# Long-convolution taps in two halves, small elementwise steps on GpSimd, two channels per table product, plain first loads

## The chip, the cores and the metric

The kernel runs on one core of a Trainium2 chip. A core has a matrix engine (TensorE, PE in the profile, with its weight loads as PEld), a vector engine (VectorE, DVE), a scalar engine (ScalarE, ACT), GpSimd (POOL), and a queue that only issues transfers (SyncE, SP). The metric is the device time of one execution in microseconds, the median of the runs.

## The reference, cut to what matters

Two layers work on the same input x of 2048 tokens by 512 channels, and a gate per token mixes them. Layer A is attention in four segments of 512 tokens with 32 heads of 16, plus a memory that is carried from segment to segment. Layer B is a state-space model that is applied as a long convolution.

```python
# A: for each of the four segments
logits = einsum('bhqd,bhkd->bhqk', qs, ks) * scale + mask
a_dot = softmax(logits) @ vs
pq = phi(qs)                       # t + 1 if t > 0 else exp(t)
a_mem = (pq @ M) / (pq @ z + 1e-6)
o = g * a_mem + (1 - g) * a_dot
M, z = M + phi(ks)^T vs, z + sum(phi(ks))
# B: taps of 2048 steps for each of 512 channels, then a convolution
P = exp(dt * A * l)
K = einsum('dn,dnl,dn->dl', Cc, P, dt * Bc).real
y = irfft(rfft(x, 4096) * rfft(K, 4096))[:2048] + x * Dskip
# mix
out = sigmoid(x . gate_w) * A(x) + (1 - sigmoid(x . gate_w)) * B(x)
```

## The kernel before

The kernel states its operations with their operands, and a planner inside it, `Sched`, gives each a place in the instruction stream of its engine. A sort key sets the order: a base key by stage plus an offset from the table `ORDER`, by the operation's tag. An operation made by `evac` may go to ACT or DVE; the planner picks one with its own costs. The streams are then fixed. Engines wait for each other by semaphores, and each stream runs in order. `MASKS` says for each of 32 groups of heads and five steps whether the causal mask is added by PE into the scores (a product with `negm`) or multiplied on DVE after the exponential.

**Start.** `praw` holds the six parameter arrays of layer B, loaded by transposing DMAs (one row of x or of a parameter becomes a column). `do_xT` loads each segment of x in the same way, in four pieces. The identity, log_dt and two weights are issued from ACT's queue (`early`).

**Powers and tables (layer B's taps).** `ssm_prep` forms z = exp(dt·A) for all channels and states, `ssm_powers` squares it again and again for ten powers and writes each as bf16 with a swapped and negated copy (lines 904 and 324/325), so that a complex product is two products and one sum. `tables(c)`, for each of four sets of 128 channels, builds a table F of 20 powers (steps 1 to 1800) and a table G of 32 powers (multiples of 8) by `cmul`, with lines 1328, 1330 and 1333 on DVE. PE then multiplies the tables over the 128 states: for each channel two matmuls (real and imaginary part) with 32 columns of G as weights and 20 of F moving, 1024 in all, four channels at once on four column strips of the array. The copies go to `kex` and by small DMAs to `KTT`, the taps.

**Attention.** For each segment and each two groups of four heads: `project` (q, k, and `ko`, a copy of k with the even heads cleared, line 1121; from segment 1 on also phi(q), lines 1125 to 1128), `seg_state` (phi(k) and the sums of the memory, lines 1075 to 1078), `group` (five steps of scores into PSUM, exponential on ACT at line 1169, mask at line 1178, products with v), `ophase` (division, lines 1229 to 1258, and a turn through DRAM for segments 0 to 2), `oproj` (output weights).

**Convolution.** `x_level1` transforms x over one part of its index and writes it to `scr_Z` in DRAM. `tail` then runs over 16 frequency groups of 128 frequencies: the taps' spectrum `PK` (five products over the five parts of the taps, for the real and for the imaginary part), copied to `K3`; the spectrum of x `PX`, copied to `Xs`; a complex product on DVE in four steps (lines 1425, 1427, 1430); the first step back `PI`, copied to `V` and by DMA into `V2`. Loads of the constants `c_D` and of `scr_Z` are issued from POOL. The last stage adds attention's part (`aj`), multiplies with `G2T` and writes the output.

Line 820 is the helper through which nearly all matmuls go, 317 that of all DMAs, 324 and 325 those of the copies on ACT and on DVE.

Of the kernel before, what the change touches and what calls it, by code (L numbers as in the profile page):

```python
# [8 lines left out]
BF16 = mybir.dt.bfloat16  # L9
# [7 lines left out]
    'c_ident': (-302.654696, 118.5323), 'c_mk': (25.0776717, 31.1201), 'c_negm': (117.240337, 15.88946),  # L17
    'c_mask': (82.9696732, 148.73681), 'c_ones': (219.06097, 69.01982), 'c_W1': (101.972009, -1.91191),
    'c_G2': (152.510402, 64.12832), 'ld0': (-159.6066, -3.90904), 'ld1': (-178.483329, -24.17737),
    'ld2': (-92.104013, -32.87557), 'ld3': (-67.6677276, 9.94046), 'ld4': (-16.8975543, -9.33976),  # L20
    'ld5': (-4.87843354, -20.81767), 'ldt': (-255.221528, 18.97994), 'ldw0.3': (-120.015437, 20.25449),
    'ldw0.4': (-107.069287, 54.02795), 'ldw0.5': (-74.7706898, 55.68128), 'ldw50': (143.580885, 71.64248),
    'ldbd': (146.873282, -3.63178), 'ldc': (75.9548493, -139.44835), 'prep': (241.088944, 76.53782),
    'xT0': (-135.794939, 94.16918), 'powA0': (-118.34783, 47.94242), 'powA1': (293.056234, 56.59733),
    'powA2': (35.605867, 26.1545), 'powA3': (85.9672701, 3.55388), 'powA4': (-134.9878, 64.48103),
    'powA5': (-26.1625064, 59.29796), 'powA6': (-133.006553, -36.0664), 'powA7': (-142.410857, 92.25773),
    'powA8': (-143.096642, 54.65219), 'powA9': (-10.832777, 2.7911), 'cbA': (-135.566534, 76.23563),
    'powB0': (-38.6484402, 86.47076), 'powB1': (5.73197339, 19.09463), 'powB2': (-13.5842481, 50.52935),
    'powB3': (-134.626625, -55.3453), 'powB4': (-158.321758, -62.26012), 'powB5': (-189.375726, 81.95324),
    'powB6': (-80.3854645, -2.33938), 'powB7': (-23.5296877, 39.40937), 'powB8': (-69.1011372, 80.90111),  # L30
    'powB9': (-110.631611, 11.18354), 'cbB': (-43.7416241, -8.34436), 'gate0': (-83.6885532, -16.32166),
    'gate': (1.11235274, 54.68591), 'proj0.0': (-19.4170356, -12.54463), 'tok0': (-79.3938344, 28.87985),
    'state0': (2.03704365, 1.9988), 'grp0.0.0': (-9.77190791, 56.39033), 'grp0.0.1': (-15.5684214, 42.32006),
    'oph0.0': (16.6476846, 20.40017), 'proj0.1': (-31.4882721, 74.16452), 'grp0.1.0': (-22.0475879, 127.40729),
    'grp0.1.1': (-23.8762151, 61.87469), 'oph0.1': (-9.68776635, -98.76067), 'proj0.2': (13.8209713, 33.73148),
    'grp0.2.0': (-3.0729207, -42.9295), 'grp0.2.1': (-4.41502647, 85.93088), 'oph0.2': (-0.110628858, -73.44253),
    'proj0.3': (-3.65051527, 62.72309), 'grp0.3.0': (-157.898249, 69.86549), 'grp0.3.1': (15.8097506, 82.05476),
    'oph0.3': (1.58288994, 45.63335), 'oproj0': (-119.328043, -32.2024), 'xT1': (152.351944, 17.87594),
    'proj1.0': (9.25225381, 119.56925), 'tok1': (-10.2534902, 33.782), 'state1': (2.65910208, -104.20105),
    'grp1.0.0': (-90.77533, -81.81367), 'grp1.0.1': (2.11773201, -114.61486), 'oph1.0': (-2.73170943, -41.40325),  # L40
    'proj1.1': (1.88542876, 58.71674), 'grp1.1.0': (-50.654272, 32.17712), 'grp1.1.1': (2.9233842, 75.51506),
    'oph1.1': (-10.8350984, -95.48593), 'proj1.2': (1.82372045, 0.09674), 'grp1.2.0': (-40.190034, 101.48513),
    'grp1.2.1': (6.26606409, 118.92692), 'oph1.2': (-0.686318884, -116.61307), 'proj1.3': (0.240651948, 30.33776),
    'grp1.3.0': (-46.8631087, 31.58558), 'grp1.3.1': (4.26113506, 92.65595), 'oph1.3': (16.5142754, -29.00959),
    'oproj1': (-191.3713, -3.8356), 'xT2': (96.7803542, 126.17717), 'proj2.0': (2.03309827, 56.77169),
    'tok2': (4.1651971, -119.61949), 'state2': (5.77674239, -0.78865), 'grp2.0.0': (-34.2653109, -9.07765),
    'grp2.0.1': (-5.67836684, 97.22657), 'oph2.0': (-250.752907, -56.23876), 'proj2.1': (6.5976729, 122.63846),
    'grp2.1.0': (-4.50294478, 30.38303), 'grp2.1.1': (4.81855669, 106.57043), 'oph2.1': (15.6722872, -167.79793),
    'proj2.2': (-0.107249989, 90.02738), 'grp2.2.0': (-195.487509, 48.11696), 'grp2.2.1': (-5.26881311, 86.02262),
    'oph2.2': (10.7493513, -113.28868), 'proj2.3': (-7.49951321, 95.76044), 'grp2.3.0': (5.83724795, 81.21215),  # L50
    'grp2.3.1': (-32.6003357, 74.62712), 'oph2.3': (-34.0930078, -105.98926), 'oproj2': (-42.4160159, -7.99807),
    'xT3': (290.268696, 20.01374), 'proj3.0': (0.804501688, 7.58942), 'tok3': (5.05705523, 9.43832),
    'grp3.0.0': (-16.6209468, 115.71971), 'grp3.0.1': (-94.3400298, 75.95984), 'oph3.0': (34.3743725, -53.14357),
    'proj3.1': (-5.34871522, 74.39357), 'grp3.1.0': (31.8837621, -11.25205), 'grp3.1.1': (-311.171354, -14.40604),
    'oph3.1': (-107.203104, -69.86356), 'proj3.2': (72.9991952, 27.09956), 'grp3.2.0': (20.1657102, -6.85936),
    'grp3.2.1': (-59.0699755, -14.4919), 'oph3.2': (88.4879918, -147.86965), 'proj3.3': (79.119397, 97.40507),
    'grp3.3.0': (5.32990942, 126.86441), 'grp3.3.1': (61.7741135, -22.60438), 'oph3.3': (-130.287319, -60.50239),
    'oproj3': (-33.6345043, -45.3022), 'tab0': (-0.0762501383, 297.60803), 'tab1': (-3.85305439, 267.74954),
    'tab2': (-0.288638216, 266.94455), 'tab3': (9.72332812, 324.53498), 'xl1': (-134.058337, -22.9888),
    'tailload': (-94.6594205, 59.19368), 'K0': (-16.3376241, 5.32994), 'K1': (44.0845545, -26.15755),  # L60
    'K2': (9.34286849, 3.42233), 'K3': (45.356053, 32.70617), 'K4': (39.7158986, -80.36254),
    'K5': (59.226848, -13.36243), 'K6': (-175.798043, 23.12264), 'K7': (-52.4250027, -83.01271),
    'K8': (-81.0202091, -26.97997), 'K9': (70.2758069, 29.6753), 'K10': (11.2349379, 25.06385),
    'K11': (-5.3357892, -30.98575), 'K12': (-72.5533468, 4.35854), 'K13': (83.6417633, 0.11429),
    'K14': (94.4918388, -109.55134), 'K15': (132.562985, 53.83523), 'fin': (-85.9153477, -15.31372),
    'pre0': (169.976104, -25.42423), 'fin0': (91.9347751, 60.72191), 'pre1': (-73.3504102, -61.54381),
    'fin1': (115.799027, 117.99035), 'fin2': (125.104546, 66.48059), 'fin3': (213.962257, 170.74892),
}
MASKS = [2, 0, 0, 0, 0, 0, 0, 0, 0, 28, 0, 0, 0, 1, 0, 0, 16, 16, 14, 4, 0, 28, 0, 1, 3, 15, 31, 31, 15, 13, 26, 20]
# [122 lines left out]
class Sched:  # L192
# [141 lines left out]
    def schedule(self):  # L334
# [23 lines left out]
        dma_free = 4.5  # L358
# [221 lines left out]

def c_mm(n, k=1):
    return k * (0.014 + n / 2300.0)
# [3 lines left out]
def fft_consts():  # L586
# [21 lines left out]
    N1 = np.zeros((128, 16, 2, 2, 64))  # L608
    for t in range(16):
        for pi in range(2):  # L610
            pp = 2 * t + pi
            c_, s_ = cs[pp].T, sn[pp].T
            rs = slice(64 * pi, 64 * pi + 64)
            N1[rs, t, 0, 0] = c_
            N1[rs, t, 1, 0] = -s_
            N1[rs, t, 0, 1] = s_
            N1[rs, t, 1, 1] = c_
    G2 = np.zeros((128, 2, 128))
    for t in range(16):
        for pi in range(2):  # L620
            for c in range(2):
                for i in range(4):
                    a_ = ang[:, 2 * t + pi]
                    G2[v2_row(t) + 4 * (4 * (pi if c == 0 else 1 - pi) + i), c, 4 * ((4 * j + i) % 32) + (4 * j + i) // 32] = 2.0 / 4096 * (np.cos(a_) if c == 0 else -np.sin(a_))
# [3 lines left out]
def v2_row(t):  # L628
    return 64 * (t >> 3) + 32 * ((t >> 2) & 1) + (t & 3)


F_EXP = [1, 3, 5, 7, 2, 4, 6, 8, 258, 260, 262, 264, 516, 520, 772, 776, 1032, 1288, 1544, 1800]
# [3 lines left out]
def dft_const():  # L636
    lq = (np_bf16_bits(np.arange(2048, dtype=np.float32)).astype(np.uint32) << 16).view(np.float32).astype(np.int64)
    where = {}
    for f, fe in enumerate(F_EXP):
        for g, ge in enumerate(G_EXP):  # L640
            assert fe + ge not in where
            where[fe + ge] = (f % 5, 4 * g + f // 5)
    assert set(lq[1:].tolist()) == set(where)
    D = np.zeros((128, 16, 5, 2, 128))
    t = np.arange(16)[:, None, None]
    pi = np.arange(2)[None, :, None]
    q = np.arange(64)[None, None, :]
    f = (2 * t + pi + 64 * q).reshape(16, 128)
    for l in range(1, 2048):
        kt, r = where[int(lq[l])]  # L650
# [922 lines left out]
```

## Time and profile before

| what | value |
|---|---|
| median of three runs | 357.27 us (355.72 to 368.35) |
| the profiled execution's own time | 355.81 us |
| its span in the profile | 354.0 us |
| mean granted PE clock | 0.946 |
| all DVE two-input table steps (lines 1328, 1330, 1333) | 52 of each, 657 ns mean |
| exponentials on ACT (line 1169) | 160, 1037 ns mean |
| mask products on DVE (line 1178) | 43, 369 ns mean |
| copies of 1024 from PSUM | 47 on ACT at 1028 ns, 16 on DVE at 1219 ns |
| copies of 512 from PSUM | 81 on ACT at 617 ns, 21 on DVE at 685 ns |
| first DVE product of the parameters | starts at 9.81 us |
| last table product on PE | about 241 us |
| last frequency group's product on DVE | ends near 332 us |

A busy share is an average over stages of different kinds, so the stages are read one by one. The time of an instruction is from its start to its end; on PE the ends are modelled, so that a burst of matmuls is better measured by its length than by the sum of its instructions. "Issue" is time in which an engine waited for nothing that the profile shows. A mean of a line covers all its sizes unless the size is given.

### The profile page before, as it was taken

How to read it: one execution, taken by the hardware profiler on the slowest of the kernel's cores; microseconds unless marked ns; L12 is line 12 of the kernel's file. 1: busy time of each engine (PE TensorE's matmuls, PEld its weight loads, DVE VectorE, ACT ScalarE, POOL GpSimd, SP SyncE). 2: the span in 40 equal slices, each digit the busy share in tenths (PEclk: the TensorE clock that was granted, in tenths of full speed). 3: DMA queues.
4: the chain of work that ended last, by engine and by line, in shares of the span. 5: the costliest groups of instructions: out<-in, count | busy, mean ns of one | idle time of the engine just before them, and what ended most of it. 6: DMA issues, size and time to landing. Idle time of an engine off the chain costs nothing.

```text
span 354.0 us, 8296 instructions
## 1 busy us (share of the span) xinstructions
PE 298.4 (84%) x3409; PEld 125.1 (35%) x3409; DVE 274.6 (78%) x667; ACT 285.9 (81%) x387; POOL 17.3 (5%) x39
## 2 busy tenths in 40 slices
PE   0669887688939999999889999987999999999691
PEld 0223332233424432543335543353343333344240
DVE  2788999999848998399998899942877778986220
ACT  2798999899937998998999898945999768665472
POOL 2000000000000000000010000000001120100000
PEclk9996999699987996999999999998999999999897
DMA  7879021013592474801006210251134656533342
GB/s 173 172 161 109 1 91 30 3 54 99 197 148 76 136 176 126 205 23 30 2 8 186 71 44 17 59 167 37 40 102 181 217 181 211 149 114 93 109 156 90
DMA packets 43117, 37.56 MB, mean 106 GB/s; under 512 B 30568, under 2 KB 35944, under 8 KB 42216
## 3 DMA queue, kind: packets, MB, share of 16 engines
q1 hardware_dynamic: 39016, 22.18, 25.8%
q0 software_dynamic: 2720, 13.63, 12.3%
q10 hardware_dynamic: 1344, 1.21, 1.5%
q8 instruction: 27, 0.44, 0.5%
q14 instruction: 10, 0.08, 0.1%
HBM read 17.74 MB, written 9.44 MB: 77 GB/s over the span
## 4 chain that ended last, share of the span: by engine, by line
DVE 38%; PE 33%; ACT 20%; issue 4%; DMA 3%; SPq 0%
PE psum L820 33%; ACT sb L1169 11%; ACT sb L324 6%; DVE sb L1330 5%; DVE sb L1328 5%; DVE sb L1333 5%; DVE sb L325 4%; DMA sb<-in_B_A_im_dram 2%; ACT sb L327 2%; DVE sb L1232 2%; DVE sb L1252 1%; DVE sb L1178 1%; DVE sb L1430 1%; DVE sb L1425 1%; DMA sb<-sb 1%
## 5 line engine op out<-in xcount | busy, mean ns | idle before, releaser
L820 PE MATMUL psum<-sb 128*32 128x20 bf16 (+13 forms) x3233 | 287.7, 276 | 46.5 <-DMA sb<-in_A_x_dram 11.7
L820 PEld LDWEIGHTS psum<-sb 128*128 128x128 bf16 (+4 forms) x3233 | 115.0, 97 | 215.2 <-issue 88.4
L1169 ACT ACTIVATE sb<-psum 128x1024 bf16<-128x1024 f32 x160 | 157.5, 1037 | 7.7 <-PE psum L820 7.1
L324 ACT ACTIVATE sb<-psum 128x512 bf16<-128x512 f32 (+2 forms) x134 | 97.7, 753 | 37.6 <-PE psum L820 36.7
L325 DVE CAST sb<-psum 128x512 bf16<-128x512 f32 (+2 forms) x39 | 34.9, 894 | 16.0 <-PE psum L820 15.8
L1328 DVE TENSOR_TENSOR sb<-sb 128x512 bf16<-128x512 bf16 (+3 forms) x52 | 34.0, 657 | 0.1
L1333 DVE TENSOR_TENSOR sb<-sb 128x512 bf16<-128x512 bf16 (+3 forms) x52 | 33.8, 658 | 0.1
L1330 DVE TENSOR_TENSOR sb<-sb 128x512 bf16<-128x512 bf16 (+3 forms) x52 | 33.6, 658 | 0.0
L1178 DVE TENSOR_TENSOR sb<-sb 128x512 bf16<-128x512 bf16 (+1 forms) x43 | 15.6, 369 | 4.6 <-ACT sb L1169 4.4
L324 ACT ACTIVATE sb<-sb 128x256 bf16<-128x256 bf16 (+1 forms) x32 | 15.4, 500 | 1.1 <-DVE sb L904 1.0
L1425 DVE TENSOR_TENSOR sb<-sb 128x1024 bf16<-128x1024 bf16 x16 | 10.8, 683 | 6.5 <-ACT sb L324 5.2
L1430 DVE TENSOR_TENSOR sb<-sb 128x512 bf16<-128x512 bf16 x32 | 13.2, 417 | 0.6
L1229 DVE RECIPROCAL sb<-psum 128x32 f32<-128x32 bf16 x16 | 5.6, 350 | 10.4 <-PE psum L1226 10.4
L317 POOL DMA_DIRECT2D sb<-c_D x16 | 8.6, 538 | 91.4 <-PE psum L820 66.5
L327 ACT ACTIVATE sb<-psum,sb 128x512 bf16<-128x512 f32 x13 | 8.6, 687 | 4.7 <-PE psum L820 4.7
L1427 DVE TENSOR_TENSOR sb<-sb 128x1024 bf16<-128x1024 bf16 x16 | 10.9, 683 | 0.2 <-ACT sb L324 0.2
L1232 DVE TENSOR_TENSOR sb<-psum,sb 128x512 bf16<-128x512 bf16 x16 | 10.9, 682 | 0.0
L1226 PE MATMUL psum<-sb 128*128 128x128 bf16 x128 | 9.8, 220 | 0.1
L1252 DVE TENSOR_TENSOR sb<-psum,sb 128x256 bf16<-128x256 f32 x24 | 9.2, 415 | 0.1
L325 DVE COPY sb<-sb 128x256 bf16<-128x256 bf16 x17 | 3.9, 247 | 6.0 <-PE psum L820 6.0
L1226 PEld LDWEIGHTS psum<-sb 128*128 128x128 bf16 x128 | 7.5, 98 | 2.5 <-ACT sb L324 0.7
L1125 ACT ACTIVATE sb<-sb 128x512 bf16<-128x512 bf16 x12 | 8.0, 666 | 0.1
(71 smaller groups left out, 142.1 us busy)
## 6 DMA issues: line engine op xcount, KB each, us to landing
sb<-c_D POOLq DMA_DIRECT2D x16, 320.0 KB, 4.4
scr_Z<-sb SPq DMA_DIRECT2D x16, 256.0 KB, 2.0
sb<-scr_Z POOLq DMA_DIRECT2D x4, 1024.0 KB, 5.5
sb<-sb SPq DMA_DIRECT2D x15, 256.0 KB
sb<-in_A_x_dram POOLq DMA_DIRECT2D x4, 512.0 KB, 5.2
scr_obuf<-sb SPq DMA_DIRECT2D x12, 128.0 KB, 1.9
scr_abuf<-sb SPq DMA_DIRECT2D x12, 128.0 KB, 1.7
sb<-scr_abuf SPq DMA_DIRECT2D x3, 512.0 KB, 6.1
```

Source lines behind the costliest of these rows:

```text
L324: fa = lambda e: e.activation(dst(), src(), ACT.Copy)
L325: fd = lambda e: e.tensor_copy(dst(), src())
L327: fa = lambda e: e.activation(dst(), src(), ACT.Copy, scale=scale())
L820: mm = lambda e, o_, l, r_, st, sp, **kw: e.matmul(o_, lhsT=l, rhs=r_, start=st, stop=sp, skip_group_check=True, **kw)
L1169: op("ACT", c_act(1024), lambda e, P=P, pT=pT: e.activation(ap(pT, n=1024), ap(P, n=1024), ACT.Exp, scale=0.25), r=[P], w=[pT])
L1178: o_ = op("DVE", c_tt(128 * len(offs)), lambda e, pT=pT, dims=dims: e.tensor_tensor(ap(pT, dims=dims + [[1, 128]]), ap(pT, dims=dims + [[1 ...
L1226: i = e.transpose(ap(P, tb * 256 + gi * 128, n=128), ap(ra[gi], tb * 128, n=128), ap(ident, n=128))
L1232: op("DVE", c_dps(512), lambda e: e.tensor_tensor(ap(o1, dims=[[128, 4], [16, 8], [1, 16]]), ap(P, dims=[[256, 4], [32, 8], [1, 16]]), ap( ...
L1328: op("DVE", ct, lambda e: e.tensor_tensor(run(tile, ne, dst, 1), run(tile, ne, src, sstep), pwv(0), ALU.mult), r=rd + [pw], w=wr + [tile])
L1330: op("DVE", ct, lambda e: e.tensor_tensor(run(t2, n, 0, 1), run(tile, ne, src, sstep), pwv(1), ALU.mult), r=rd + [pw], w=[t2])
L1333: op("DVE", max(c_tt(256 * n), 0.4), lambda e: e.tensor_tensor(D_(), D_(), ap(t2, n * 128, [[-n * 128, 2], [2 * n, 64], [1, 2 * n]]), ALU. ...
L1430: op("DVE", c_tt(512), lambda e, Y=Y, Tt=Tt, c=c, alu=alu: e.tensor_tensor(ap(Y, 512 * c, n=512), ap(Y, 512 * c, n=512), ap(Tt, 512 * c, n ...
```

## The change

1. **First loads.** A_re, A_im and the first segment of x come by plain DMAs and are transposed on PE; the two weights that were issued from ACT's queue are issued from SP's.
2. **Copies, minima and maxima on GpSimd.** The negated and the swapped copy of each power, `ko`, the clips of phi(q) and phi(k), the first entries of the tables, and the second product of `cmul` where it makes one or two powers.
3. **Tables and their products.** F is ordered by odd and even steps. One matmul takes 64 columns of G (two neighbouring channels) as weights and 40 of F; of its 64×40 results the two blocks of a channel with itself are kept. 512 matmuls in three pieces for each set of channels.
4. **Taps to frequency.** Frequency f and the one half a period on have the same sums over even taps and opposite sums over odd taps. So the even part (`PK[0]`, four products) and the odd part (`PK[1]`, four) are formed once for two groups; their sum and their difference are two DVE steps from PSUM and SBUF. `tail` runs over eight double groups; its four DVE steps become two of 2048 and two of 1024; the constants N1, D and G2 are ordered to suit.
5. **Masks and filler.** `MASKS` has 81 steps on DVE where it had 43. `FILLS` puts one unused 128×512 matmul ahead of the scores in 55 steps.
6. **Order.** All of `ORDER` is new, and with it the choice of ACT or DVE for the copies.

```diff
-MASKS = [2, 0, 0, 0, 0, 0, 0, 0, 0, 28, 0, 0, 0, 1, 0, 0, 16, 16, 14, 4, 0, 28, 0, 1, 3, 15, 31, 31, 15, 13, 26, 20]
+MASKS = [0, 1, 2, 3, 0, 20, 11, 24, 15, 24, 11, 9, 10, 8, 15, 19, 21, 17, 4, 21, 16, 29, 17, 1, 27, 23, 31, 31, 31, 30, 14, 24]
+FILLS = [0, 3, 10, 3, 0, 23, 27, 4, 4, 4, 8, 7, 19, 16, 9, 10, 14, 25, 2, 12, 0, 0, 22, 0, 10, 4, 0, 0, 6, 10, 29, 26]
...
-F_EXP = [1, 3, 5, 7, 2, 4, 6, 8, 258, 260, 262, 264, 516, 520, 772, 776, 1032, 1288, 1544, 1800]
+F_EXP = [1, 3, 5, 7, 2, 6, 258, 262, 4, 8, 260, 264, 516, 520, 772, 776, 1032, 1288, 1544, 1800]
...
+            if wi < 2:
+                S.dma(lambda T=T: ap(T, n=512), lambda wi=wi: prm[wi].rearrange("(p k) n -> p (k n)", k=4), 131072, w=[T], key=(-1.6, -1.7)[wi])
...
+                        for k in range(4):
+                            i = e.transpose(ap(P, t2 * 512 + k * 128, n=128), ap(xks, (2 * hb + t2) * 512 + k * 128, n=128), ap(ident, n=128))
...
-                op("DVE", c_ts4(256), lambda e, dst=dst: e.tensor_scalar(dst(384, 1), dst(256, 1), -1.0, None, ALU.mult), r=parts, pw=parts)
-                S.evac(lambda dst=dst: dst(0, 1), lambda dst=dst: dst(128, 1), 256, r=parts, pw=parts, sb=True)
+                op("POOL", c_pl(256), lambda e, dst=dst: e.tensor_scalar(dst(384, 1), dst(256, 1), -1.0, None, ALU.mult), r=parts, pw=parts)
+                op("POOL", c_pl(256), lambda e, dst=dst: e.tensor_copy(dst(0, 1), dst(128, 1)), r=parts, pw=parts)
...
-            op("DVE", c_ts4(512), lambda e: e.tensor_scalar_min(ap(ek, n=512), ap(ek, n=512), 1.0), w=[ek])
+            op("POOL", c_pl(512), lambda e: e.tensor_scalar_min(ap(ek, n=512), ap(ek, n=512), 1.0), w=[ek])
...
+                    if FILLS[gidx] >> si & 1:
+                        mm(e, ap(P, n=512), ap(kT, n=128), ap(qT, n=512), True, True)
...
-                op("DVE", ct, lambda e: e.tensor_tensor(run(t2, n, 0, 1), run(tile, ne, src, sstep), pwv(1), ALU.mult),
+                op(*(("POOL", c_pl2(256 * n)) if n < 3 else ("DVE", ct)), lambda e: e.tensor_tensor(run(t2, n, 0, 1), run(tile, ne, src, sstep), pwv(1), ALU.mult),
...
-                                    i = mm(e, ap(P, sl * NF, n=NF, p0=32 * dq, np_=32), ap(G, (1 - cc) * GPL + (dl // 2) * 2 * NG + dl % 2, [[2, NG]]),
-                                           ap(F, cc * FPL + (dl // 2) * 2 * NF + dl % 2, [[2, NF]]), cc == 0, cc == 1, tile_position=(0, 32 * dq))
+                                    i = mm(e, ap(P, sl * 2 * NF, n=2 * NF, p0=64 * ct, np_=64), ap(G, (1 - cc) * GPL + j * 2 * NG + par, [[2, 2 * NG]]),
+                                           ap(F, cc * FPL + j * 2 * NF + par, [[2, 2 * NF]]), cc == 0, cc == 1, tile_position=(0, 64 * ct))
...
-                        for kt in range(5):
-                            i = mm(e, ap(PK, c * 512, n=512), ap(Dt, kt * 256 + c * 128, n=128), ap(KTT, kt * 32, [[160, 16], [1, 32]]), kt == 0, kt == 4)
+                            for k in range(4):
+                                kt = k + 1 if eo == 0 or k else 0
+                                i = mm(e, ap(PK[eo], c * 512, n=512), ap(Dt, (4 * eo + k) * 256 + c * 128, n=128), ap(KTT, kt * 32, [[160, 16], [1, 32]]), k == 0, k == 3)
...
+                S.evac(lambda Es=Es: ap(Es, n=1024), lambda PK=PK: ap(PK[0], n=1024), 1024, r=[PK[0]], w=[Es])
+                for h in range(2):
+                    op("DVE", c_dps(1024), lambda e, h=h, K3=K3, PK=PK, Es=Es: e.tensor_tensor(
+                        ap(K3, 1024 * h, n=1024), ap(Es, n=1024), ap(PK[1], n=1024), ALU.subtract if h else ALU.add), r=[Es, PK[1]], pw=[K3])
...
-                op("DVE", c_tt(1024), lambda e, Y=Y, Xs=Xs, K3=K3: e.tensor_tensor(ap(Y, dims=[[512, 2], [1, 512]]), ap(Xs, dims=[[512, 2], [1, 512]]),
-                                                                                 ap(K3, dims=[[0, 2], [1, 512]]), ALU.mult), r=[Xs, K3], w=[Y])
+                op("DVE", c_tt(2048), lambda e, Y=Y, X_=X_, K_=K3: e.tensor_tensor(
+                    ap(Y, dims=[[1024, 2], [512, 2], [1, 512]]), ap(X_, dims=[[1024, 2], [512, 2], [1, 512]]),
+                    ap(K_, dims=[[1024, 2], [0, 2], [1, 512]]), ALU.mult), r=[X_, K3], w=[Y])
```

## The prediction

> **What bounds the kernel now.** I read the busy table first, then the chain of waits, then a table of stages, and last the waits and the timeline where a stage stood idle.
>
> ```profile
> PE 298.4 (84%) x3409; PEld 125.1 (35%) x3409; DVE 274.6 (78%) x667; ACT 285.9 (81%) x387; POOL 17.3 (5%) x39
> ```
> ```profile
> DVE 38%; PE 33%; ACT 20%; issue 4%; DMA 3%; SPq 0%
> ```
>
> Three engines are about 80% busy and share the chain; POOL is empty. No single engine decides over the whole span, so it has to be read by stage (columns: stretch, length, then busy us of PE, PEld, DVE, ACT, POOL, then PE clock):
>
> ```profile
> 94.00:114.00 20.00, 14.20 (x298) 6.34 (x287) 13.02 (x33) 11.81 (x17) 0.53 (x1) 0.83 0.61 128
> 114.00:134.00 20.00, 18.63 (x170) 8.24 (x166) 20.00 (x38) 19.32 (x25) 0.53 (x1) 1.00 0.57 149
> 134.00:156.00 22.00, 21.19 (x416) 9.43 (x416) 14.10 (x43) 20.10 (x27) 1.06 (x2) 0.84 0.53 141
> 156.00:180.00 24.00, 21.23 (x195) 8.44 (x194) 24.00 (x46) 22.17 (x31) 0.66 (x2) 1.00 0.05 12
> ...
> 226.00:246.00 20.00, 16.36 (x385) 8.65 (x381) 8.34 (x30) 11.38 (x20) 0.54 (x1) 0.91 0.32 95
> ...
> 296.00:320.00 24.00, 23.18 (x194) 9.40 (x196) 20.62 (x39) 16.91 (x18) 1.61 (x3) 1.00 0.45 134
> ```
>
> Stage A (0 to 26) waits for first loads. In stage B (26 to 246: attention, tables) DVE is full while it builds tables (114 to 134, 156 to 180) and idle where PE multiplies them (94 to 114, 134 to 156, 226 to 246). By stage B's seven stretches DVE is busy 189 of 220 us, ACT 193. In stage C (246 to 332, the tail's frequency blocks) PE is full. The rest is the output. Why the product stretches are empty:
>
> ```profile
> PE psum L820 <- issue: 8.5, 3, 4.8
> ```
> ```profile
> 98.35 1.22 PEld L820 LDWEIGHTS psum<-sb 128*32 128x32 bf16 x128 [0.59 <-issue]
> 104.82 0.14 PEld L820 LDWEIGHTS psum<-sb 128*32 128x32 bf16 x8 [5.25 <-issue]
> 105.26 0.13 PEld L820 LDWEIGHTS psum<-sb 128*128 128x128 bf16 x2 [0.30 <-issue]
> 105.67 0.15 PEld L820 LDWEIGHTS psum<-sb 128*128 128x128 bf16 x1 [0.28 <-issue]
> ```
>
> PE ran 128 tiny products at 10 ns each, then stood 4.8 us with nothing to wait for; the second long gap (3.1 us, to 240.65) follows 236 of them. I read these as PE running out of fetched instructions. After the gap the big loads come 0.43 us apart, twice the 0.216 us of the chain's "3.68 PE x17" at 66.76: the clock has dropped (PEclk 0.83 here).
>
> **What the Trainium skill says.** (1) "SBUF — State Buffer", Who interferes with whom: a DVE instruction with two SBUF inputs contends with a GpSimd instruction that reads SBUF; whoever comes first holds the shared port for its whole instruction. This trace shows no such pair, since POOL only clears memory and issues DMAs. (2) "GPSIMD Engine Reference", Elementwise: about 1.03 cycles an element at 1.2 GHz with one input, 2.6 with two. Not in this trace. (3) The same page, Instruction dispatch: the first call of a freshly loaded GpSimd kernel costs some 6 us unseen. The changed POOL stream has one more set-up instruction (ISA) ahead of its first negation; no run here shows its cost yet. (4) "TensorE: Matmul & The Clock Gate", Part 1: an idle array falls to half clock until it has been busy some microseconds. The 0.43 against 0.216 us agrees.
>
> **The change part by part** (counts are those of the two instruction streams).
>
> *First loads.* A_re, A_im and the first x tile come by plain DMA and 24 PE transposes instead of DMA transposes; weights move from ACT's queue to SP's. DVE now starts at 9.81, when A_im lands 7.7 us after its issue. The plain 128 KB log_dt load took 4.1 us. Gain 3.6, less transposes and a strided PSUM copy (two steps of about 0.6): −2.5. Bounds −4 to +2, the loss if wq, now fifth on SP behind the x loads, lands after x.
>
> *DVE relieved (stage B).* To POOL go 20 negations (20×215 ns = 4.3), ko 16×346 = 5.5, minima and maxima 12×(285+318+288) = 10.7, 17 copies×247 = 4.2. The second product of the 1- and 2-step table powers goes too: table DVE falls from 102.6 to 89.5 (the counts of L1328, L1330 and L1333 by their means, 0.41 to 1.21), 13.1. Added: 81 mask products instead of 43, 34 of the 38 more in stage B, ×0.36 = 12.2. Evacuations: 12 more of 512 (+8.2), 7 fewer of 1024 (−8.5). Net 37.8−12.2 = **−25** of DVE. ACT loses 23 copies (9.8) and 10 evacuations of 512 (6.2), gains some 3: −13.
>
> *POOL loaded.* 52 one-input operations of 512, 60 of 256, 24 two-input of 512, 12 of 256. By the skill's cycles the streaming is 52×0.44+60×0.22+24×1.11+12×0.55 = 69 us; with the 0.41 us that clearing 15 elements takes here (second line, four times) for dispatch,
>
> ```profile
> L1042 POOL MEMSET sb<- 128x128 bf16 x4 | 2.5, 704 | 19.7 <-PE psum L820 19.7
> ...
> L1043 POOL MEMSET sb<- 128x15 bf16 x4 | 1.7, 414 | 0.0
> ```
>
> estimated 130 us. Under 300, so POOL is no bound, and a slow first call is covered: the negations are first read by tables near 20. Behind each now wait what a 0.29 us DVE step fed: the DVE add of a minimum, the scores that use ko; and the tail's D and Z loads queue behind minima. Scores are prepared a group ahead, so I cost this latency at nothing.
>
> *The port.* About 65% of DVE's work has two SBUF inputs (tables 89, masks 29, f32 squarings, state sums). If every POOL instruction held DVE for its whole length, 130×0.65 = 85 us; if DVE always came first, 0. Part of each POOL instruction is dispatch, POOL waits too, and some waits fall into DVE's idle 31 us: I take 0.65×69 = 45, and somewhat under half of it, **+20**, called C below. Bounds 0 and 45 for the range, 85 as the rival's extreme.
>
> *Products.* 512 matmuls of 64×40 replace 1024 of 32×20, so a burst is half as many instructions. PE's own time here was 10 to 15 ns each, small. What I count is the stalls: 6 of the 8.5 us, and 2 of the slow clock after them: −8 (0 to −14). The 55 added filler matmuls cost PE 55×0.216 = 12 us in stages where it is 85 to 96% busy, and the masks moved to DVE give back 36×0.053+40×0.107 = 6; I let the remainder go against a better held clock (−6 to +6).
>
> *The new order* can't be priced from this trace. At best it fills idle time (DVE 31 us, ACT 27 in stage B), and an order planned without the port's waits can open as much; I take 0 and leave it to the range.
>
> Stage B: −25+20−8 = −13. ACT's floor for it is −13−6 = −19 (its removed work and the stalls).
>
> *Tail.* PE: the even and odd halves need 128 matmuls instead of 160: −32×0.216 = −6.9. X and output products keep their array time. DVE: per old pair of blocks 2×(2×0.683+2×0.417) = 4.4; now 2 PSUM adds of 1024 (about 1.22, as the PSUM cast), 2 of 2048 at 1.21, 2 of 1024 at 0.68: 6.2. Over 8 blocks +14.6, against 8 fewer evacuations. DVE was busy 67 of stage C's 86 us, so it becomes about as full as PE was: what PE gives is taken by DVE, with one K3, Es and Tt buffer. At the end the V2 copies of two blocks come together, +1 at most. I take −1 (−6 to +7).
>
> Sum: −2.5−13−1 = −16.5, so a span of 337.5. The profiled execution took 355.8 for 354.0, and the median of the runs is 357.3, 1.5 above: 337.5+1.8+1.5 = **341**.
>
> **The rivals.** *The port is free* (0.17): DVE's dedicated port serves it, C is 0, and ACT's floor holds: −2.5−19−3 gives about 333. For it: every DVE duration here is steady. Against: only the skill speaks on it.
>
> *The port is a lock* (0.22), the slower side: DVE, full in stage B, is held by about 130 POOL instructions. At C = 45: −2.5−25+45−8−1 = +8.5, 366; at 85 about 406. It turns slower than +2% from C = 44, a third of a microsecond for each of 148 operations. For it: DVE is exactly the engine that is full in 114 to 134 and 156 to 226. Against: POOL waits as well.
>
> *Given back* (0.11): gaps were not the burst's fault (DMA was over 90% busy then[...]), the filler takes PE time, the tail's single buffers serialize: the −8 falls to 0 and the tail rises to +5: 355.
>
> **How the numbers follow.** The likeliest has 0.5 (0.43 of it beyond 2%). Faster 0.43+0.17 = 0.60; same 0.07+0.10 = 0.17; slower 0.22+0.01 = 0.23. Two per cent, 350 to 364, is what a measurement of this kernel can tell from no change. Range: from all good ends together (about −30, 326) to the lock at C = 45 (366), 325 to 367.
>
> **What will show it.** The table steps of L1328 and L1333 and the masks of L1178 keep 0.41, 0.68 and 1.21 us if the port is free, and have longer means or gaps put to POOL if not. POOL busy near 130. "PE <- issue" under 3 us. Table stretches on DVE shorter. Tail with DVE over 90% busy. First DVE product near 7.3. I am wrong if POOL instructions take over 1.5 us each, or if the groups wait for POOL in their place.

## The result and the profile after

| | before | after |
|---|---|---|
| median of five runs each, us | 357.27 (353.08 to 368.35) | 393.14 (388.95 to 396.10) |
| ratio, 95% interval | | 1.100 (1.086 to 1.114) |
| the profiled execution, us | 355.81 | 396.10 |
| its span, us | 354.0 | 394.3 |
| granted PE clock in it | 0.946 | 0.864 |
| last table step of 2048 on DVE ends, us | 228.1 | 253.1 |

The change makes the kernel 10% slower. I had predicted 341 us, with a range of 325 to 367. Executions of one kernel differ by some per cent together with the granted clock; the ratios here compare the faster ones of both kernels, and the profiled execution of the changed kernel (396.10 us) is one of its slower ones, so its PE clock of 0.864 is on the low side (0.88 to 0.89 in the faster ones).

First the busy table and the chain of waits of the changed kernel:

```profile
PE 325.6 (83%) x2932; PEld 132.4 (34%) x2932; DVE 315.1 (80%) x583; ACT 280.6 (71%) x357; POOL 187.3 (48%) x183
...
DVE 42%; PE 36%; POOL 9%; ACT 6%; issue 3%; DMA 3%; SPq 0%; DVEq 0%
```

DVE runs 84 instructions fewer than before (583 for 667) and is busy 40 us longer (315.1 for 274.6). Work was taken from it, so its instructions must have become longer. POOL is now 9% of the chain, some 35 us, and ACT has fallen from 20% to 6%.

The groups of DVE by shape (busy us, mean ns of one, idle time before them) show which instructions became longer. Lines 1371, 1373 and 1376 are the table steps (1328, 1330 and 1333 before), 1221 the masks (1178 before), 328 the copies. First some groups of the kernel before, then those of the changed one:

```profile
L325 DVE CAST sb<-psum 128x512 bf16<-128x512 f32 x21 | 14.4, 685 | 8.8 <-PE psum L820 8.8
...
L1333 DVE TENSOR_TENSOR sb<-sb 128x512 bf16<-128x512 bf16 x16 | 6.6, 415 | 0.0
L1328 DVE TENSOR_TENSOR sb<-sb 128x512 bf16<-128x512 bf16 x16 | 6.6, 410 | 0.0
...
L1178 DVE TENSOR_TENSOR sb<-sb 128x256 bf16<-128x256 bf16 x16 | 4.6, 285 | 2.0 <-ACT sb L1169 1.8
```

```profile
L328 DVE CAST sb<-psum 128x512 bf16<-128x512 f32 x32 | 21.9, 684 | 12.7 <-PE psum L828 12.5
...
L1371 DVE TENSOR_TENSOR sb<-sb 128x512 bf16<-128x512 bf16 x24 | 16.3, 680 | 0.2
L1376 DVE TENSOR_TENSOR sb<-sb 128x2048 bf16<-128x2048 bf16 x12 | 16.0, 1331 | 0.0
...
L1376 DVE TENSOR_TENSOR sb<-sb 128x512 bf16<-128x512 bf16 x24 | 13.1, 546 | 0.0
L1221 DVE TENSOR_TENSOR sb<-sb 128x256 bf16<-128x256 bf16 x34 | 12.4, 369 | 0.8 <-ACT sb L1212 0.8
...
L1275 DVE TENSOR_TENSOR sb<-psum,sb 128x512 bf16<-128x512 bf16 x16 | 10.8, 676 | 0.2
```

A table step of 512 took 410 to 420 ns before and takes 680 and 546 now; a mask of 256 went from 285 to 369. Copies and products with an input in PSUM stand where they were (684 for 685 before). A slower DVE would stretch all of them. What is stretched has its inputs in SBUF, and nearly all of it has two.

Then POOL's own durations:

```profile
L1373 POOL TENSOR_TENSOR sb<-sb 128x512 bf16<-128x512 bf16 x24 | 32.9, 1373 | 29.9 <-DVE sb L1376 29.8
L1160 POOL TENSOR_SCALAR sb<-sb 128x512 bf16<-128x512 bf16 x16 | 27.1, 1696 | 7.6 <-ACT sb L327 6.5 <-DVE sb L328 0.9
L1116 POOL TENSOR_SCALAR sb<-sb 128x512 bf16<-128x512 bf16 x12 | 21.0, 1751 | 3.8 <-ACT sb L1114 3.6
L943 POOL TENSOR_SCALAR sb<-sb 128x256 bf16<-128x256 bf16 x20 | 20.5, 1030 | 25.1 <-ACT sb L327 20.9 <-DVE sb L328 4.1
```

What DVE did in 0.29 us (`ko` in 0.35) takes POOL 1.7. I had estimated 0.85 for these, and POOL busy 130 us in all; it is 187. How DVE comes to wait for such an instruction is seen in the timelines of DVE and then of POOL (start, length, what ended the idle time):

```profile
121.71 0.41 DVE L1371 TENSOR_TENSOR sb<-sb 128x256 bf16<-128x256 bf16 x1
123.08 0.42 DVE L1115 TENSOR_SCALAR sb<-psum 128x512 bf16<-128x512 bf16 x1 [0.96 <-ACT sb L1114]
124.97 0.42 DVE L1117 TENSOR_TENSOR sb<-sb 128x512 bf16<-128x512 bf16 x1 [1.47 <-POOL sb L1116]
```
```profile
121.90 1.58 POOL L1160 TENSOR_SCALAR sb<-sb 128x512 bf16<-128x512 bf16 x1 [0.86 <-DVE sb L328]
123.46 1.49 POOL L1116 TENSOR_SCALAR sb<-sb 128x512 bf16<-128x512 bf16 x1
```

The minimum of line 1116 was placed behind a ko of line 1160 on POOL's stream, so DVE's add stands 1.47 us for it.

The trace thus offers two theories. **The lock**: a POOL instruction that touches SBUF holds DVE. **The wait**: streams run in order, and now stand for slow POOL results. The rival to both is that POOL is not to blame: masks, fillers, the new tail or the new order.

### The profile page after: what moved, and what is told of

It reads as the page before. It is cut to its first block, busy times and chain, and to the rows that moved or that the text cites. A ratio compares the mean times of both kernels' runs of the same rounds, so it can differ in the third digit from the quotient of the medians.

```text
span 394.3 us, 7392 instructions
## 1 busy us (share of the span) xinstructions
PE 325.6 (83%) x2932; PEld 132.4 (34%) x2932; DVE 315.1 (80%) x583; ACT 280.6 (71%) x357; POOL 187.3 (48%) x183
## 4 chain that ended last, share of the span: by engine, by line
DVE 42%; PE 36%; POOL 9%; ACT 6%; issue 3%; DMA 3%; SPq 0%; DVEq 0%
PE psum L828 34%; DVE sb L1376 6%; DVE sb L1371 6%; DVE sb L328 5%; ACT sb L327 4%; DVE sb L1461 4%; DVE sb L1221 4%; DVE sb L1373 3%; POOL sb L1116 2%; DVE sb L1473 2%; DVE sb L1476 2%; ACT sb L1212 2%; POOL sb L1160 2%; DVE sb L1480 2%; DMA sb<-sb 1%
## 5 line engine op out<-in xcount | busy, mean ns | idle before, releaser
L828 PE MATMUL psum<-sb 128*128 128x512 bf16 (+15 forms) x2732 | 310.5, 322 | 50.8 <-DVE sb L1221 10.4
L327 ACT ACTIVATE sb<-psum 128x512 bf16<-128x512 f32 (+6 forms) x127 | 94.6, 756 | 64.7 <-PE psum L828 62.4
L1373 POOL TENSOR_TENSOR sb<-sb 128x512 bf16<-128x512 bf16 (+1 forms) x36 | 41.5, 1160 | 30.2 <-DVE sb L1376 29.8
L328 DVE CAST sb<-psum 128x512 bf16<-128x512 f32 (+3 forms) x44 | 34.0, 774 | 17.2 <-PE psum L828 17.0
L1371 DVE TENSOR_TENSOR sb<-sb 128x512 bf16<-128x512 bf16 (+3 forms) x56 | 44.2, 797 | 0.3
L1376 DVE TENSOR_TENSOR sb<-sb 128x512 bf16<-128x512 bf16 (+3 forms) x56 | 41.3, 745 | 1.0 <-POOL sb L1373 0.9
L1221 DVE TENSOR_TENSOR sb<-sb 128x512 bf16<-128x512 bf16 (+1 forms) x81 | 33.9, 428 | 7.3 <-ACT sb L1212 7.3
L943 POOL TENSOR_SCALAR sb<-sb 128x256 bf16<-128x256 bf16 x20 | 20.5, 1030 | 25.1 <-ACT sb L327 20.9
L1160 POOL TENSOR_SCALAR sb<-sb 128x512 bf16<-128x512 bf16 x16 | 27.1, 1696 | 7.6 <-ACT sb L327 6.5
L1165 POOL TENSOR_SCALAR sb<-sb 128x512 bf16<-128x512 bf16 x12 | 20.4, 1707 | 20.9 <-ACT sb L327 19.6
L1166 POOL TENSOR_SCALAR sb<-sb 128x512 bf16<-128x512 bf16 x12 | 20.0, 1671 | 9.7 <-ACT sb L1164 9.6
L1461 DVE TENSOR_TENSOR sb<-sb,psum 128x1024 bf16<-128x1024 f32 x16 | 18.9, 1214 | 5.6 <-PE psum L828 5.6
L1116 POOL TENSOR_SCALAR sb<-sb 128x512 bf16<-128x512 bf16 x12 | 21.0, 1751 | 3.8 <-ACT sb L1114 3.6
L1373 DVE TENSOR_TENSOR sb<-sb 128x2048 bf16<-128x2048 bf16 (+1 forms) x20 | 20.7, 1037 | 0.0
```

The costliest lines, as they stand in the source:

```text
L327: fa = lambda e: e.activation(dst(), src(), ACT.Copy)
L328: fd = lambda e: e.tensor_copy(dst(), src())
L828: mm = lambda e, o_, l, r_, st, sp, **kw: e.matmul(o_, lhsT=l, rhs=r_, start=st, stop=sp, skip_group_check=True, **kw)
L1116: op("POOL", c_pl(512), lambda e: e.tensor_scalar_min(ap(ek, n=512), ap(ek, n=512), 1.0), w=[ek])
L1160: op("POOL", c_pl(512), lambda e: e.tensor_scalar(ap(ko, n=512), ap(kT, n=512), ap(mkT, n=1), None, ALU.mult), r=[kT, mkT], w=[ko])
L1221: o_ = op("DVE", c_tt(128 * len(offs)), lambda e, pT=pT, dims=dims: e.tensor_tensor(ap(pT, dims=dims + [[1, 128]]), ap(pT, dims=dims + [[1 ...
```

## Experiments: POOL's part

Nearly all kernels here keep the changed kernel's order as it was planned, and only then move or drop instructions, so that a comparison isn't blurred by a new plan. Line numbers of their traces are one or a few higher than those of the changed kernel. Times are medians; each ratio is to the kernel before, run beside it on the same chip.

**All on DVE.** After the planning, the 148 element operations of POOL become DVE's:

```diff
         S.schedule()
+        moved = [o for o in S.order if kind(o) in MOVE]
+        for o in moved:
+            o.eng = "DVE"
```

> The changed kernel with all 148 element operations that it gives to POOL (52 minima, maxima and ko, 60 negations and copies, 36 second products) issued on DVE at the same places of its order; PE, ACT and the DMA queues keep their streams. Lock theory (DVE is held while POOL reads SBUF): DVE's table steps return to 0.41, 0.60 to 0.68 and 1.21 us, DVE busy is near 267+42 = 309, and the time is near 393-45+20 = 355 to 368. Latency theory (the streams, each in order, wait for slow POOL results): 393-34 = 355 to 365, some 34 us of POOL being on the chain. Rival (fillers, more masks on DVE, the tail and the new order cost the time, not POOL): 385 to 400.

368.0 us, ratio 1.022 (1.010 to 1.034): 25 us less than the changed kernel, and DVE is busy 305.2 us, with the table steps of 512 back at 421 to 427 ns. So POOL is to blame for most of the loss, by one way or the other. But 368 is still above the kernel before, where the prediction's other terms leave about nothing; the second set of experiments asks why.

**Unused work on POOL.** With everything on DVE, POOL gets at each of the 148 places an instruction that nobody needs: of the same kind, reading a constant (`all_plus_reads`), or a clearing, which only writes (`all_plus_sets`).

```diff
+            h.eng, h.inc, h.waits = "POOL", False, []
+            h.alld = list(o.alld) + W1w + shadows[-4:-3]
+            shadows.append(h)
+            new.append(h)
```

> all_on_dve, and at each of the 148 places an added POOL instruction of the same kind and length, which reads a constant from SBUF, writes a scratch tile and is waited for by nobody. Lock theory: the table steps stretch again as in the changed kernel (0.41 to 0.60 and more), DVE busy rises by 35 to 50 us and the time by 25 to 48 us over all_on_dve. Latency theory: within 2% of all_on_dve, since nobody waits for these instructions. Rival (neither): within 2% too.

> all_on_dve, and at each of the 148 places a POOL memset in place of the reading instruction: it writes SBUF only, is waited for by nobody. Lock by POOL's reads: within 2% of all_on_dve with table steps unstretched. If any POOL access to SBUF holds DVE: the same stretch as with the reads, +25 to 48 us. Latency theory and the rival: within 2%.

414.3 us, 1.154 (1.146 to 1.162), and 415.5 us, 1.158 (1.150 to 1.167). Nobody waits for these instructions, and they cost 46 and 48 us over `all_on_dve`. The lock is shown, and its price: with the reads DVE is busy 350.1 us for 305.2, that is 44.9/148 = 0.30 us for each POOL instruction. One other way is left open by the edit: POOL also issues loads, and these now stand behind the unused work. But then DVE would stand idle for longer, and it doesn't (60.7 us of the span with the reads, 63.0 without). My expectation that clearing costs nothing was wrong. The groups by shape tell why. First `all_on_dve` (table step 1374, ko 1161, the copy 945 and the maximum 1167), then with the reads, then with the clearings:

```profile
L1374 DVE TENSOR_TENSOR sb<-sb 128x512 bf16<-128x512 bf16 x24 | 10.1, 421 | 0.0
...
L1161 DVE TENSOR_SCALAR sb<-sb 128x512 bf16<-128x512 bf16 x16 | 6.1, 383 | 0.0
...
L945 DVE COPY sb<-sb 128x256 bf16<-128x256 bf16 x20 | 4.5, 225 | 0.0
...
L1167 DVE TENSOR_SCALAR sb<-sb 128x512 bf16<-128x512 bf16 x12 | 3.4, 286 | 0.0
```
```profile
L1374 DVE TENSOR_TENSOR sb<-sb 128x512 bf16<-128x512 bf16 x24 | 17.2, 716 | 0.0
...
L945 DVE COPY sb<-sb 128x256 bf16<-128x256 bf16 x20 | 6.5, 323 | 0.0
...
L1167 DVE TENSOR_SCALAR sb<-sb 128x512 bf16<-128x512 bf16 x12 | 4.8, 402 | 0.0
```
```profile
L945 DVE COPY sb<-sb 128x256 bf16<-128x256 bf16 x20 | 16.6, 832 | 0.1
L1161 DVE TENSOR_SCALAR sb<-sb 128x512 bf16<-128x512 bf16 x16 | 15.8, 986 | 0.0
L1167 DVE TENSOR_SCALAR sb<-sb 128x512 bf16<-128x512 bf16 x12 | 15.1, 1255 | 0.0
...
L1374 DVE TENSOR_TENSOR sb<-sb 128x512 bf16<-128x512 bf16 x24 | 10.0, 416 | 0.0
```

With reads DVE's products with two SBUF inputs are longer (421 to 716), and less so its one-input instructions in bf16 (286 to 402, 225 to 323). Clearings leave the products of line 1374 alone (416) and hold the one-input instructions far longer (286 to 1255, 225 to 832). Some other two-input groups are longer with clearings too (the sum of line 1118: 421 to 509); in the timeline their long ones lie beside a one-input instruction that is held (at 54.60 a copy takes 1.08 us, the sum that starts at 54.73 ends with it). One such meeting, in the timelines of DVE and of POOL in `all_plus_sets`:

```profile
158.92 0.42 DVE L1222 TENSOR_TENSOR sb<-sb 128x512 bf16<-128x512 bf16 x1
159.25 0.69 DVE L1377 TENSOR_TENSOR sb<-sb 128x1024 bf16<-128x1024 bf16 x1
159.86 1.50 DVE L1167 TENSOR_SCALAR sb<-sb 128x512 bf16<-128x512 bf16 x1
```
```profile
159.40 1.80 POOL L1606 MEMSET sb<- 128x2048 bf16 x1 [3.86 <-ACT sb L1165]
```

The clearing runs from 159.40 to 161.20. A two-input sum of 1024 passes beside it in its usual 0.69 us; the maximum of 512, usually 0.29 us, starts at 159.86 and is done at 161.36, just after the clearing. The Trainium skill, "SBUF — State Buffer", Who interferes with whom, says both: two-input products contend with GpSimd's reads and not with its writes, and copies and `tensor_scalar` in their fast two-port modes contend with GpSimd altogether. Both agree with these numbers. I had used only the first half of it.

**Only the 52 operations of 512 back** (`MOVE = ('clip',)`), and **only the second products left on POOL** (`MOVE = ('clip', 'pow', 'copy')`):

> The changed kernel with only the 52 minima, maxima and ko products of 512 back on DVE at the same places; 96 operations stay on POOL. They take 83 of POOL's 187 us and some 22 of the 34 us that POOL has on the chain. Latency theory: about two thirds of the gain of all_on_dve, 370 or below. Lock theory: their share of POOL's time, 0.45 of the gain of all_on_dve less the 15 us that DVE takes back, 375 to 385. Rival: 385 to 400.

> The changed kernel with only the 36 second products of the table steps left on POOL; minima, maxima, ko, negations and copies are on DVE, in the same order. Lock: 36x0.3 = 11 us of DVE held against 14 us taken from it, 364 to 370, as all_on_dve. If waiting for 1.4 us on POOL in place of 0.42 on DVE counts, since the add right behind needs it: 371 to 378.

376.5 us, 1.050 (1.041 to 1.059), and 381.9 us, 1.056 (1.044 to 1.069). The first time lies in the range named for the lock (375 to 385) and above that for the wait (370 or below), though the share of the gain, two thirds, is the one that the wait theory had; the 52 are 89 of POOL's 187 us (lines 1116, 1160, 1165, 1166). By itself that run doesn't decide. The second result lies above both ranges: 36 products, 48 us on POOL (24 of 1.60 us and 12 of 0.82), cost 3% over `all_on_dve`, though DVE gave away 15 us. Even the products that POOL does best don't pay. Its trace also shows the other side of the lock: one product of 512 on POOL took 6.82 us (from 68.53), while DVE ran ten instructions at their usual lengths between 68.69 and 74.39. So POOL is held too, and the products' mean of 1.60 contains it.

**The wait by itself.** 128 of the operations are left out of the computation. In one kernel (`nobody_waits`) POOL runs unused reads in their places, in the other (`left_out`) nothing. Consumers then wait for what the left-out operation waited for, and read zeros or older values. From the first to the second the only difference is that POOL is idle. From the changed kernel to the first nobody waits, and two things come with the edit: other values in the data, and five clearings at the head of DVE's stream (6.3 us), behind which DVE's first product starts at 11.06 us and not at 7.66.

```diff
+        drop(moved)
+        S.order = inits + S.order
```

> The changed kernel with 128 of its POOL operations (52 minima, maxima and ko, 40 negations and copies of the powers, 36 second products; the 20 table copies stay) left out of the computation, and in the place of each a POOL instruction of the same kind and length that reads a constant and is waited for by nobody. POOL is as busy as in the changed kernel and DVE has the same work. Lock theory: DVE's steps stay stretched, DVE busy near 315, and the time stays with the changed kernel's, 385 to 396. Latency theory: the 34 us of POOL on the chain fall out, 360 to 370. If both count, with the reads' 46 us as the lock: 368-38+46 = 376 to 382, so the waits cost some 12 to 18 us.

> The same 128 operations left out of the computation and nothing in their place, so POOL keeps only the 20 table copies: what the change would give if POOL's share cost nothing. The prediction's own terms without the port: 357-2.5-25-8-1 and the copies, near 325 to 333. If the tail and the added masks cost more than I counted, as all_on_dve at 368 suggests: 368 less most of the 38 us that DVE no longer has, 335 to 350.

| kernel | median us | ratio (95%) | DVE busy us, profiled | PE clock, profiled |
|---|---|---|---|---|
| changed | 393.1 | 1.100 (1.086 to 1.114) | 315.1 | 0.864 |
| nobody_waits | 387.6 | 1.075 (1.061 to 1.090) | 319.7 | 0.903 |
| left_out | 345.9 | 0.964 (0.954 to 0.975) | 281.2 | 0.982 |

The lock is 387.6 − 345.9 = 41.7 us by the medians and 40 by the ratios, and again (319.7 − 281.2)/128 = 0.30 us of DVE for each POOL instruction. DVE's idle time hides none of it: 58.5 us of the span in `left_out`, 60.4 in `nobody_waits`. The waits are 393.1 − 387.6 = 5.5 us by the medians, 9 by the ratios, and between 2 and 16 by the intervals; up to 3.4 us more, if DVE's later start carries through to the end, which no run here tells, nor what the other values do. The trace of the changed kernel agrees with the size: DVE's idle time that a POOL result ended is 6.7 us in all, 5.8 of it at the two kinds of sums behind minima, and PE's is 0.2 (the columns are us in total, times, longest).

```profile
DVE sb L1117 <- POOL sb L1116: 3.7, 4, 1.5
...
DVE sb L1167 <- POOL sb L1166: 2.1, 3, 1.1
...
PEld psum L828 <- POOL sb L1160: 0.2, 1, 0.2
```

So the 35 us that POOL has on the chain were no measure of what waiting costs. My reading is that where POOL's result comes sooner, a held DVE ends the same wait. The chain names who was last, not what is gained without him.

The clock falls with it. The rows of granted clock of `left_out` and of `nobody_waits` (forty slices, 9 is 90% or more):

```profile
PEclk9999999999999999999999999999999999997796
```
```profile
PEclk9996996795599969996995998989999999999898
```

With POOL at work PE waits 9.7 us for DVE's masks instead of 2.0, its clock is 0.903 instead of 0.982, and for the same matmuls it is busy 307.6 us instead of 283.5 (those of 128x512 over the whole array take 417 ns in the mean for 396). That the pauses lower the clock is not tested here; the fillers below, which fill pauses and raise it, speak for it.

## Experiments: what remained

`all_on_dve` is 2% above the kernel before. Four edits of it, and one of the kernel before, ask for the part.

**Masks.** 47 of the 81 masks go back to PE, those whose slot the kernel before has there (`KEEP` is its `MASKS`), and their DVE products are dropped:

```diff
+            if m is not None and m[2] == -1 and not KEEP[m[0]] >> m[1] & 1:
+                MD[m[0], m[1]] = False
+                gone.append(o)
```

> all_on_dve (368.0), with 47 of the 81 mask products taken from DVE and made by PE's -30000 matmuls instead, as the kernel before does for these slots; same order otherwise. DVE loses 47x0.36 = 17 us, PE gains some 4. If DVE's load is what all_on_dve has over the kernel before: 355 to 362. If the tail is: 364 to 369.

367.8 us, 1.026 (1.015 to 1.038). DVE is busy 292.8 us for 305.2, and no gain is seen. One of some 4 us could hide in the intervals; the 6 to 13 us that I had named for DVE's load could not.

**Fillers.** The 55 matmuls without a use are left out of `all_on_dve`, or put into the kernel before:

```diff
-                    if FILLS[gidx] >> si & 1:
+                    if FILL_ON and FILLS[gidx] >> si & 1:
                         mm(e, ap(P, n=512), ap(kT, n=128), ap(qT, n=512), True, True)
```

> all_on_dve (368.0) without the 55 filler matmuls, whose result nobody uses; same order otherwise. PE loses 55x0.216 = 12 us. If they only take PE's time: 358 to 365. If they hold PE's clock, as I let them cancel in the prediction: 366 to 375, with more slices below 9 in the row of granted clocks.

> The kernel before with the changed kernel's 55 filler matmuls, at the same groups and steps, nothing else. If fillers hold PE's clock here too, as all_on_dve against no_fillers shows (8.5 us): 348 to 354. If they only take PE's time: 55x0.216 = 12 us on PE, of which stage B hides some: 358 to 368.

376.5 us, 1.041 (1.031 to 1.051), and 358.9 us, 1.003 (0.998 to 1.007). The fillers are worth some 7 us in `all_on_dve` by the ratios (8.5 by the medians; the intervals allow 1 to 12) and nothing in the kernel before.

**The tail.** In the traces the stretch after the last table step of 2048 is 137 us in `all_on_dve` and 126 before, so I suspected the new tail and put the old one back, with its constants and buffers:

```diff
-            for u in range(8):
-                S.key = k0 + 4 + 2 * dk * u
+            for t in range(16):
+                S.key = k0 + 4 + dk * t
...
```

> all_on_dve (368.0) with the tail of the kernel before: sixteen blocks of one pair, 160 frequency products, no even and odd halves, double K3 and Tt buffers; the tables, their products over two channels, the first loads, masks and fillers stay as in the changed kernel. The order is kept up to two thirds of the tables and differs a little after. If the new tail costs what the stage lengths say (137 us after the last table against 126): 357 to 361. If it is neutral, as I predicted with -1: 366 to 370.

370.3 us, 1.032 (1.027 to 1.037): no gain. The stage's length had misled me: 40 exponentials lie after that step against 31 before, so attention's work had only moved into the tail.

**The end.** In the last stage of `all_on_dve` 41 matmuls took 10.98 us, where 42 took 9.24 before. They read V2 in runs of two.

```diff
-ap(V2, (b4 * 2 + kt) * 512, [[2, 128], [256, 2], [1, 2]])
+ap(V2, (b4 * 2 + kt) * 512, n=512)
```

> all_on_dve (368.0), the final products reading V2 in runs of 512 elements instead of runs of two (the channels then come out in another order). In the changed kernel 42 of the last matmuls take 12.75 us, in all_on_dve 41 take 10.98, before 42 took 9.24. If the short runs slow the array: 366 or below by 1.5 us, and the last stage's matmuls return to 0.22 us each. If it is the clock alone: no change.

364.6 us, 1.015 (1.010 to 1.021). The total is 3.4 us lower, which the intervals don't tell from nothing, and not where it should be: the last stage's 42 matmuls still took 10.93 us, at a clock of 0.82, and the last table step of 2048, which the edit doesn't touch, ended 2.5 us earlier. The short runs cost nothing that this shows.

**The order.** What is left is that the order was made for operations on POOL. The planner gets the same work with no element operation on POOL, and a new table `ORDER` was searched for it. The choice of engine for the copies is part of it: 24 of the 40 copies of 256 come to lie on ACT here (30 in the third kernel), where `all_on_dve` and `old_tail` have them on DVE. The kernels are: with the old tail and 48 masks (`new_order_old_tail`), the same with the 55 fillers added (`new_order_fillers`), and with the new tail and 58 masks (`new_order_new_tail`).

```diff
-            op("POOL", c_pl(512), lambda e: e.tensor_scalar_min(ap(ek, n=512), ap(ek, n=512), 1.0), w=[ek])
+            op("DVE", c_ts4(512), lambda e: e.tensor_scalar_min(ap(ek, n=512), ap(ek, n=512), 1.0), w=[ek])
...
```

> The work of old_tail (all element operations on DVE, the changed kernel's first loads and two-channel table products, the tail of the kernel before) without fillers and with 48 mask products on DVE, in an order that the kernel's planner has made for exactly this work, where old_tail (370.3) and all_on_dve (368.0) run an order that was made with these operations on POOL. If that order is what they have over the kernel before (359): the first loads (-2.5) and products (-8) come through, 345 to 352. If another part of the change costs it: 362 to 370.

> new_order_old_tail with the changed kernel's 55 filler matmuls at the same groups and steps, nothing else moved. As in before_fillers, no difference beyond 1%, if PE has few pauses; up to 8 us faster, as from no_fillers to all_on_dve, if it has as many as there.

> The same with the changed kernel's tail (even and odd halves), 58 mask products on DVE, no fillers, in an order made for exactly this work, with less time given to finding it. If the order is the cause: clearly below all_on_dve (368) and no_fillers (376), 352 to 360. If the new tail or the masks are: 364 to 376.

| kernel | median us | ratio (95%) |
|---|---|---|
| new_order_old_tail | 359.9 | 1.0005 (0.996 to 1.005) |
| new_order_fillers | 350.6 | 0.973 (0.968 to 0.978) |
| new_order_new_tail | 366.7 | 1.030 (1.016 to 1.043) |

`old_tail`, with fillers, has 1.032; the same work in its own order, with fillers, has 0.973. That is 20 us for the order, with the copies on ACT and the 33 fewer masks on DVE in it (the masks moved back showed no gain in the experiment above; the copies were not tried alone). Without fillers the first of the three misses my 345 to 352, and the second shows what it lacked: 9.3 us of fillers. `new_order_new_tail`, without fillers too, is 10 us under `no_fillers` by the medians, but 4 by the ratios, and their intervals overlap: with the new tail an own order is not shown to gain anything. It lies where I had put it if the new tail or the masks were to blame. `old_tail` speaks against that, and its order had less searching; which of the two it is stays open. The rows of granted clock, without fillers (an execution of 367.7 us) and with them (347.6 us); over all twenty executions of each the median clock is 0.90 and 0.96:

```profile
PEclk9999655899855799987987998599999999999788
```
```profile
PEclk9995999999899999999999999999999999999698
```

`new_order_fillers` is the version that beats both kernels: the change's plain loads, two-channel products and fillers, with the old tail and no element operation on POOL.

## Why the prediction was wrong, step by step

**The port, +20: this step failed.** "Part of each POOL instruction is dispatch, POOL waits too, and some waits fall into DVE's idle 31 us", so I took somewhat under half of 45. The mechanism, its place and even its price per instruction were in the rival (a third of a microsecond for each of 148; measured 0.30). The lock costs 40 to 42 us between `left_out` and `nobody_waits`, near the upper bound that I had set for the range, and two reasons for halving it went wrong. No part of it fell into DVE's idle time, which is 58.5 us without the lock and 60.4 with it. And POOL's one-input instructions of 512 take 1.7 us for the estimated 0.85: the cycles for one input that the prediction took over don't hold for these, where the measurement decides, so the exposure is larger. That POOL waits too is seen (the product of 6.82 us); what that saved is not measured. The part of DVE that I had counted was nearly right: shape by shape, the changed kernel's DVE instructions are 37 us longer than those of `left_out`, and 34 of it is in those with two inputs in SBUF. The hold on one-input instructions, which I had not counted, matters in the runs that keep these on DVE. The sign that I had named for the lock, table steps with longer means, came true.

**"Scores are prepared a group ahead", latency at nothing: mis-sized.** The waits are 5 to 9 us by `nobody_waits`, perhaps some more. The scores themselves hardly wait (PE 0.2 us for `ko`); DVE's adds behind the minima do. That POOL's operations take over 1.5 us was my own condition for being wrong.

**DVE relieved, −25: its worth depends on the order.** From `all_on_dve` to `left_out` DVE loses 128 operations in the same order, and the time falls by 22 us. But `new_order_fillers` (0.973), where DVE and ACT do all of them, is within noise of `left_out` (0.964). My reading is that a fitting order puts most of that work into DVE's idle time. And of the +12.2 of added masks nothing is seen: 47 of them back on PE moved the time by 0.2 us.

**The new order, taken as 0: mis-sized, in part argued.** With the old tail an order made for the engines in use is 20 us better than one made for others; with the new tail no gain is shown.

**Fillers against clock, 0: mis-sized.** −7 to −10 in the two kernels whose clock is low without them (0.87 and 0.90), 0 in the kernel before; my −6 was close to the former.

**The products' stalls, −8, and first loads, −2.5: not measured by themselves.** What the trace was to show is there. The row "PE <- issue" is gone, and the first DVE product of the parameters starts at 7.66 us (9.81 before; I said near 7.3). But `new_order_old_tail`, which has both and no fillers, only equals the kernel before (1.0005); the 2.7% of `new_order_fillers` come with the fillers. So whether the stalls were worth 8 us stays open, and their cause too: the rival's full DMA engines fit the first long gap of the kernel before (a DMA share above 0.9 from 100.0 to 104.8) and not the second (0.38 from 237.5 to 240.7).

**Tail, −1: right** as far as `old_tail` tells (370.3 for 368.0). DVE over 90% busy in it was wrong: 35.0 of 43 us in one of its stretches in the changed kernel.

Together: the terms without the port gave −36.5, or −24.5 with the floor that I had set for ACT; `left_out` has −13 by its ratio (up to 3 us less without its clearings). The lock adds 40, where I had 20, and the waits 9, where I had none, which makes +36; that this is the measured change is no test, since the three steps lead from one kernel to the other. How the 11 us by which even the floor was missed divide among the terms is not settled: `left_out` runs a planned order whose worth I can't part from that of the relief, and reads other values.

## What to carry to other kernels

Before moving elementwise work to an idle GpSimd, count what it does to VectorE: here each GpSimd instruction held VectorE for 0.30 us, as much as most of the moved instructions cost there (0.22 to 0.42), and what needed its result had to wait up to 1.7 us for it. Here an engine that looked idle was not free, because its accesses to memory held another. Where an order is fixed by a planner, judge a change with a plan made for it, and distrust both the share on the chain and a stage's length until work is counted on both sides of the stage's border.

## What the runs showed of the hardware that I had not expected

A clearing on POOL, which reads nothing, holds DVE's bf16 `tensor_scalar` and copies with one SBUF input (0.29 to 1.26 us, 0.23 to 0.83) and leaves two-input products at 0.42. DVE holds POOL as well (one product of 6.82 us). A one-input `tensor_scalar` of 512 bf16 elements on POOL takes 1.67 to 1.75 us in the mean and never less than 1.48, a product of two inputs 1.37 in the mean: the simpler one is the slower. And 55 matmuls that compute nothing make a kernel whose PE pauses 9.3 us faster (359.9 to 350.6), while the kernel before doesn't notice them.
